# ScalarE's order in an opening attention, four weights loaded together, and query groups moved nearer to their keys

## The chip, the cores and the metric

The kernel runs on one core of one Trainium2 chip. Its time is the device time of one execution in microseconds (us). TensorE multiplies into PSUM banks (PE; PEld is its weight load), VectorE (DVE) and ScalarE (ACT) read the banks and work in SBUF, GpSimd (POOL) does little here, and SyncE (SP) issues most DMAs. Each engine takes its own instructions in a fixed order and waits at one until what it needs is there.

## The reference

Three stages follow one another: a linear attention over 4 batches of 8 heads, 576 positions and 64 dimensions, and two MLPs over the 2304 tokens.

```python
def phi(x):                                    # x: q or k of one head, w_phi 64x128
    proj = x @ w_phi
    proj = proj - max(abs(proj), axis=-1)
    return concat([exp(proj), exp(-proj)])     # 256 features
num = phi(q) @ (phi(k).T @ v);  den = phi(q) @ sum(phi(k)) + 1e-6
x = num / den                                  # heads side by side: 2304 x 512
h = x @ w_in;    x = max(0.01 * h, h) @ w_out  # 512 -> 2048 -> 512
g = x @ w_gate;  out = (silu(g) * (x @ w_val)) @ w_out2   # 512 -> 1536 -> 512
```

The inputs are laid out on the host, and the weights come as 64-bit floats of which a DMA brings the raw words.

## The kernel before

**Batches and units.** The work goes batch by batch. The MLPs of a batch are a list of units, each of 24 matmuls or so (`u_l1`, `u_out`, `u_gate`, `u_val`); the attention of batch b + 1 is mixed into the units of batch b. Only the attention of batch 0 has nothing to be mixed into. It is the opening, and it is what the change is about: TensorE, ScalarE and VectorE work on it alone, with a few weight conversions and the first matmuls of the first units, which can start before the last quarter of x is there.

**The opening.** Heads go in pairs, j = 0 to 3. The keys of a pair come in three groups (`first_k`: two matmuls per 128 positions into one bank, VectorE's largest absolute value L434, VectorE's difference, and on ScalarE the two exponentials L439 and L440). Then `first_back` multiplies them with the values into one bank (L218), and at the pair's last group ScalarE copies that bank to SBUF as `kvh` (`k_z`, L63). The queries of a pair come in two halves t of 288 positions, so there are eight query groups: `q_p` (projection L332, and VectorE's transposed maximum L337), `q_m_t` (a transposition L349 and a short chain on VectorE that ends in the row of maxima L362), `q_exp` (L372 subtracts it in the bank, ScalarE's exponentials L374 and L375, for two heads), `q_num` (L392, two matmuls per head with `kvh`, after which ScalarE takes the denominator `dn`, L395), and `q_fin` (VectorE: transpose L400, reciprocal L402, transpose L404, two products L410 to `xf`; then ScalarE's rounding to `xh`, L63, and VectorE's rest `xl`). x of the batch is there when the `xl` of the eighth group is written.

**Weights.** A weight tile takes three steps. `w_load` brings 512 KB into one of five `wi` buffers. `w_to_f32` makes a 32-bit float of it: on ScalarE L563 and L564, on VectorE L572, L573 and L578. `w_split` rounds it on ScalarE (L588) and takes the rest on VectorE (L60). The result is again a `wi` tile (first layer) or a `wo` tile (second layer). `split_next` does this for the next weight in the order of need, with two conversions and up to five loads ahead. The order of need is: four weights of the first layer, then the first of the second layer, the fifth of the first layer, and the other three of the second layer for the first `u_out`.

**What sets the order.** The program calls the steps of the opening in the order of the times that `first_steps` gives them, but a scheduler then orders the instructions of each engine by its own estimates. A stamp (`stamp_issue_order_token`) keeps the instructions that carry the same token in the order of the program. In the kernel before, the rounding of weights, the matmuls of units and some loads are stamped, and nothing of the opening is.

## Time and profile before

| | us |
|---|---|
| median of 3 runs (lowest, highest) | 1082.61 (1078.01, 1087.24) |
| the profiled execution | 1085.46 |
| its span, first to last instruction | 1083.5 |
| mean granted clock of TensorE in it | 0.987 of full speed |

The profiled execution is 2.85 us above the median. Rows of a timeline give the start in us, the length in us, engine and line, what is written and read, how many instructions were merged into the row, and in brackets how long the engine had sat idle and for whom. A row that merges several pipelined instructions is longer than the time until the next one starts. A 32-bit matmul leaves two records. Windows give busy us of each engine in a stretch, instructions in brackets, and the share of full speed that TensorE's clock was granted.

### The profile page before, as it was taken

What the parts mean: (1) busy time and instruction counts of PE and PEld (TensorE: products, weight loads), DVE (VectorE), ACT (ScalarE), POOL (GpSimd) and SP (SyncE); (2) the same over time, 40 slices, a digit from 0 to 9 for tenths busy, and PEclk for the clock granted to TensorE, in tenths of its full rate; (3) what the DMA queues carried; (4) which work ended last, traced back from release to release, by engine and by line L of the source; (5) the groups of instructions that cost most, each with busy time, mean ns of one, the idle gap of its engine ahead of it and who ended that gap; (6) DMA issues with size and microseconds to landing.
All of it is one profiled execution on the core that took longest, in us unless ns stands there. A gap on an engine that the chain in (4) does not pass through costs nothing.

```text
span 1083.5 us, 20399 instructions
## 1 busy us (share of the span) xinstructions
PE 1052.4 (97%) x7642; PEld 1025.2 (95%) x7642; DVE 795.2 (73%) x1730; ACT 648.9 (60%) x1443; POOL 21.7 (2%) x57
## 2 busy tenths in 40 slices
PE   8689999999999999999999999999999999999998
PEld 7579999998989999999999989999999999999998
DVE  5876778899898988968686855958878732368473
ACT  4656979788887787756563466754544334336541
POOL 1000100000000000000000000000000000000000
PEclk9699999999999999999999999999999999999999
DMA  7523677657665786786463385536977757657542
GB/s 221 182 60 125 223 261 257 235 186 243 211 230 192 287 341 239 262 305 238 164 224 127 121 318 205 186 117 258 320 250 280 287 193 275 219 175 273 207 141 86
DMA packets 101490, 236.17 MB, mean 218 GB/s; under 512 B 19856, under 2 KB 35984, under 8 KB 101392
## 3 DMA queue, kind: packets, MB, share of 16 engines
q1 hardware_dynamic: 94560, 219.41, 58.4%
q0 software_dynamic: 4032, 14.68, 3.4%
q8 instruction: 60, 0.98, 0.4%
q10 hardware_dynamic: 2800, 0.79, 0.3%
q14 instruction: 38, 0.31, 0.1%
HBM read 169.30 MB, written 65.54 MB: 217 GB/s over the span
## 4 chain that ended last, share of the span: by engine, by line
PE 61%; DMA 6%; DVE 3%; ACT 2%; issue 1%; SPq 0%; DVEq 0%
PE pm L652 42%; PE pa L778 8%; PE pm L778 4%; PE pa L392 2%; PE pa L230 2%; DMA wi<-parts 1%; DMA wi<-in_w_dram 1%; DMA wr<-kept 1%; PE pa L177 1%; DMA sums<-wr 1%; DMA wi<-in_wg_dram 0%; DMA vhl<-parts 0%; PE pa L372 0%; DVE xl L60 0%; PE pa L271 0%
## 5 line engine op out<-in xcount | busy, mean ns | idle before, releaser
L652 PE MATMUL pm<-xh,wi 128*128 128x288 f32 x1664 | 354.6, 300 | 3.1 <-DVE wi L60 1.0
L652 PE MATMUL pm<-gp,wo 128*128 128x288 f32 x2256 | 339.3, 296 | 1.5 <-ACT es L680 0.6
L652 PEld LDWEIGHTS pm<-gp,wo 128*128 128x128 f32 x2256 | 311.8, 188 | 3.4 <-ACT es L680 1.1
L652 PEld LDWEIGHTS pm<-xh,wi 128*128 128x128 f32 x1664 | 271.9, 188 | 7.7 <-DVE wi L60 2.2
L652 PE MATMUL pm<-xl,wi 128*128 128x288 f32 x832 | 246.5, 297 | 0.0
L652 PEld LDWEIGHTS pm<-xl,wi 128*128 128x128 f32 x832 | 156.7, 188 | 0.7
L719 DVE TENSOR_TENSOR acc<-pm,acc 128x288 f32<-128x288 f32 x160 | 70.2, 451 | 46.6 <-PE pm L652 45.8
L60 DVE TENSOR_TENSOR gp<-es,gp 128x576 fp32r<-128x576 f32 x94 | 70.4, 749 | 26.1 <-ACT gp L63 25.6
L63 ACT ACTIVATE gp<-es 128x576 fp32r<-128x576 f32 x94 | 64.6, 687 | 29.5 <-DVE es L700 24.4
L60 DVE TENSOR_TENSOR wi<-wr,wi 128x512 fp32r<-128x512 f32 x96 | 64.9, 683 | 12.0 <-ACT wi L588 11.3
L588 ACT ACTIVATE wi<-wr 128x512 fp32r<-128x512 f32 x96 | 60.0, 636 | 17.9 <-DVE wr L60 5.1
L778 PE MATMUL pm<-xh,wi 128*128 128x288 f32 x272 | 62.5, 296 | 2.1 <-DMA wi<-parts 1.2
L563 ACT ACTIVATE wr<-wi 128x512 f32<-128x512 f32 x68 | 46.3, 686 | 22.4 <-DMA wi<-in_w_dram 11.4
L60 DVE TENSOR_TENSOR fl<-ff,fh 128x512 fp32r<-128x512 f32 (+1 forms) x72 | 51.1, 712 | 11.2 <-ACT fh L63 10.8
L564 ACT ACTIVATE wi<-wi 128x512 int32<-128x512 uint32 x68 | 46.8, 688 | 18.2 <-DMA wi<-in_w_dram 12.4
L578 DVE TENSOR_TENSOR wr<-wr,wi 128x512 uint16<-128x512 uint16 x68 | 51.0, 750 | 0.8
L778 PEld LDWEIGHTS pm<-xh,wi 128*128 128x128 f32 x272 | 46.4, 188 | 3.2 <-DVE mk L182 1.2
L395 ACT ACTIVATE dn<-pa 64x288 f32<-64x288 f32 x64 | 26.0, 407 | 38.0 <-PE pa L392 37.2
L63 ACT ACTIVATE fh<-ff 128x512 fp32r<-128x512 f32 (+1 forms) x72 | 47.2, 659 | 0.9
L680 ACT ACTIVATE es<-pm 128x288 f32<-128x288 f32 x72 | 29.7, 418 | 27.2 <-PE pm L778 16.6
L63 ACT ACTIVATE acc<-pm 128x288 f32<-128x288 f32 x64 | 26.7, 431 | 25.5 <-PE pm L652 25.3
L700 DVE SCALAR_TENSOR_TENSOR es<-pm,es 128x288 f32<-128x288 f32 x72 | 32.2, 448 | 11.6 <-PE pm L652 11.1
(212 smaller groups left out, 2083.3 us busy)
## 6 DMA issues: line engine op xcount, KB each, us to landing
wo<-parts SPq DMA_DIRECT2D x77, 512.0 KB, 6.1
wi<-parts SPq DMA_DIRECT2D x68, 512.0 KB, 6.0
parts<-wi SPq DMA_DIRECT2D x56, 512.0 KB, 4.5
wi<-in_w_dram SPq DMA_DIRECT2D x44, 512.0 KB, 4.4
wr<-kept SPq DMA_DIRECT2D x64, 256.0 KB, 4.2
parts<-wo POOLq DMA_DIRECT2D x28, 512.0 KB, 5.4
kept<-wr SPq DMA_DIRECT2D x40, 256.0 KB, 4.5
wi<-in_wg_dram SPq DMA_DIRECT2D x12, 512.0 KB, 4.3
```

The lines of the kernel that those rows point to most:

```text
L60: dve.tensor_tensor(out=o, in0=a, in1=b, op=ALU.subtract)
L63: act.activation(o, a, AF.Copy)
L395: act.activation(dn[b, j, t][D * h : D * h + D], ps[D:P], AF.Copy, bias=1e-6)
L563: act.activation(t, high.bitcast(F32), AF.Abs, scale=REBIAS)
L564: act.activation(low, low.bitcast(U32), AF.Copy, scale=2.0**-29)
L578: dve.tensor_tensor(out=t16, in0=t16, in1=e16, op=ALU.add)
L588: i = act.activation(t[:, 0], r, AF.Copy)
L652: m = pe.matmul(ps, w, x[:, c], start=(i == 0), stop=(i == n - 1))
L680: act.activation(o, i, AF.Prelu, alpha=0.01)
L700: dve.scalar_tensor_tensor(out=g[:, c], in0=ps, scalar=0.5, in1=g[:, c], op0=ALU.mult, op1=ALU.mult)
L719: dve.tensor_tensor(out=acc[o][:, t], in0=ps, in1=acc[o][:, t], op=ALU.add)
L778: m = pe.matmul(ps, a, b, start=start and n == 0, stop=stop and n == 5, skip_group_check=True)
```

## The change

Instructions of ScalarE in the opening get one token, `opening`: every copy, exponential and denominator of the attention, and the first instruction of each weight conversion (L563 before, L570 now). So ScalarE takes these in the program's order. The second instruction of a conversion (L564, now L572) gets none. The first four weights are loaded together behind the last queries, with none further ahead, and each `split_first` converts and splits one weight; four are converted in the opening. The program's times are moved: the keys' products come 1.1 steps sooner after their exponentials, the query groups start one step earlier and follow at 1.3 steps, and their own steps lie nearer together. The first queries and the constants are loaded ahead of the second keys.

```diff
--- before.py
+++ after.py
@@ -59,8 +59,14 @@
     def sub(o, a, b):
         dve.tensor_tensor(out=o, in0=a, in1=b, op=ALU.subtract)
 
+    opening = [True]
+
+    def in_opening(i):
+        if opening[0]:
+            tc.stamp_issue_order_token(i.ins, "opening")
+
     def cp(o, a):
-        act.activation(o, a, AF.Copy)
+        in_opening(act.activation(o, a, AF.Copy))
 
 
     cst_sb = const.tile([P, NC], F32, name="cst_sb")
@@ -162,7 +168,8 @@
         v = vraw.pop((b, j))
         vhl[b, j] = t = T([P, NST, 2, 2, D], F32R, "vhl", 1)
         for st in (slice(0, 2), slice(2, NST)):
-            cp(t[:, st, :, 0, :], v[:, st])
+            i = act.activation(t[:, st, :, 0, :], v[:, st], AF.Copy)
+            tc.stamp_issue_order_token(i.ins, "opening")
             sub(t[:, st, :, 1, :], v[:, st], t[:, st, :, 0, :].bitcast(F32))
 
     def k_front(b, j, s):
@@ -371,8 +378,8 @@
         r = mrow[b, j][:, NB * t : NB * t + NB].rearrange("p k i -> p (k i)")
         pe.matmul(ps, sel[:, h], r, start=False, stop=True, skip_group_check=True)
         f = T([P, 2, HT], F32, "ff" if b else ("ff", "fh", "fl")[(2 * t + h + j) % 3], 3)
-        act.activation(f[:, 0], ps, AF.Exp)
-        act.activation(f[:, 1], ps, AF.Exp, scale=-1.0)
+        in_opening(act.activation(f[:, 0], ps, AF.Exp))
+        in_opening(act.activation(f[:, 1], ps, AF.Exp, scale=-1.0))
         if whole(b):
             qfh[b, j, h, t] = f
             return
@@ -392,7 +399,7 @@
             pe.matmul(ps, w, x, start=(i == 0), stop=(i == len(ops) - 1))
         if h == 0:
             dn[b, j, t] = T([P, HT], F32, "dn", 2)
-        act.activation(dn[b, j, t][D * h : D * h + D], ps[D:P], AF.Copy, bias=1e-6)
+        in_opening(act.activation(dn[b, j, t][D * h : D * h + D], ps[D:P], AF.Copy, bias=1e-6))
 
     def q_fin(b, j, t):
         d = dn.pop((b, j, t))
@@ -436,8 +443,8 @@
         d = f.rearrange("p n h a f -> p (n h) a f")
         m = mk.rearrange("p (r o) -> p r o", o=1).to_broadcast([P, 2 * n, F])
         sub(d[:, :, 1], pv, m)
-        act.activation(d[:, :, 0], d[:, :, 1], AF.Exp)
-        act.activation(d[:, :, 1], d[:, :, 1], AF.Exp, scale=-1.0)
+        in_opening(act.activation(d[:, :, 0], d[:, :, 1], AF.Exp))
+        in_opening(act.activation(d[:, :, 1], d[:, :, 1], AF.Exp, scale=-1.0))
         for i in range(n):
             ff[0, j, s + i] = f[:, i]
 
@@ -456,15 +463,15 @@
 
         for i, (j, s, n) in enumerate(pairs):
             at(i, first_k, j, s, n)
-            at(i + 2.5, first_back, j, s, n)
+            at(i + 1.4, first_back, j, s, n)
         for g in range(2 * NP):
             j, t = divmod(g, 2)
-            base = 3 + 1.25 * g
-            last = max(base + 2.4, 3 * j + 4.6 + 0.4 * t)
+            base = 2 + 1.3 * g
+            last = max(base + 2.05, 3 * j + 3.5 + 0.4 * t)
             at(base + 0.1, q_p, 0, j, t)
-            at(base + 0.9, q_m_t, 0, j, t)
+            at(base + 0.7, q_m_t, 0, j, t)
             for h in range(2):
-                at(base + 1.5 + 0.2 * h, q_exp, 0, j, h, t)
+                at(base + 1.25 + 0.1 * h, q_exp, 0, j, h, t)
                 at(last + 0.2 * h, q_num, 0, j, h, t)
             at(last + 0.25, q_fin, 0, j, t)
         steps = [[] for _ in range(int(max(e[0] for e in events)) + 1)]
@@ -560,7 +567,8 @@
         low, high = r[:, :, 0], r[:, :, 1]
         t = T([P, 512], F32, "wr", 4)
         ti = t.bitcast(I32)
-        act.activation(t, high.bitcast(F32), AF.Abs, scale=REBIAS)
+        i = act.activation(t, high.bitcast(F32), AF.Abs, scale=REBIAS)
+        tc.stamp_issue_order_token(i.ins, "opening")
         act.activation(low, low.bitcast(U32), AF.Copy, scale=2.0**-29)
         if key[0] in "gv3":
 
@@ -1072,6 +1080,10 @@
         for k in slots[i]:
             split_next()
 
+    def split_first():
+        ahead(conv, w_to_f32, done[0] + 1)
+        ahead(done, w_split, done[0] + 1)
+
 
     atts = {}
 
@@ -1093,27 +1105,29 @@
 
     warm_up()
     load_k(0, 0)
+    load_q(0, 0)
+    load_constants()
     load_k(0, 1)
-    load_q(0, 0)
+    load_q(0, 1)
     load_k(0, 2)
-    load_constants()
-    load_q(0, 1)
+    load_q(0, 2)
     load_k(0, 3)
-    load_q(0, 2)
     steps = first_steps()
 
     for i, todo in enumerate(steps):
         for fn in todo:
             fn()
-        if i == 2:
+        if i == 1:
             query_constants()
-        if i == 5:
+        if i == 4:
             load_q(0, 3)
-        if i in (6, 8, 10, 12):
-            split_next()
-        if i == 13:
+            ahead(loaded, w_load, 4)
+        if i in (4, 6, 8, 10):
+            split_first()
+        if i == 11:
             split_constants()
             load_k(1, 0)
+    opening[0] = False
     for i in range(NU):
         units[i]()
         splits(i)
```

Three places of ScalarE's order show what moves. Line numbers of the changed kernel are a few higher.

The first is ScalarE at the first query group, from its last exponentials to the next group's. `wr` and `wi` rows are conversions, `vhl` copies of values for the fourth batch, `dn` the first group's denominators, `wo` exponentials of keys. Before:

```order
L374 ACTIVATE fh_237<-pm_193 128x288
L375 ACTIVATE fh_237<-pm_193 128x288
L563 ACTIVATE wr_355<-wi_351 128x512
L564 ACTIVATE wi_351<-wi_351 128x512
L563 ACTIVATE wr_363<-wi_353 128x512
L564 ACTIVATE wi_353<-wi_353 128x512
L63 ACTIVATE vhl_4429<-vraw_3723 128x4x64
L588 ACTIVATE wi_371<-wr_355 128x512
L63 ACTIVATE vhl_4429<-vraw_3723 128x6x64
L395 ACTIVATE dn_257<-pa_254 64x288
L395 ACTIVATE dn_257<-pa_274 64x288
L374 ACTIVATE fl_292<-pm_220 128x288
```

Now:

```order
L381 ACTIVATE fh_216<-pm_184 128x288
L382 ACTIVATE fh_216<-pm_184 128x288
L69 ACTIVATE kvh_223<-pa_160 128x512
L572 ACTIVATE wi_293<-wi_293 128x512
L446 ACTIVATE wo_236<-wo_236 128x4x128
L447 ACTIVATE wo_236<-wo_236 128x4x128
L402 ACTIVATE dn_249<-pa_246 64x288
L402 ACTIVATE dn_249<-pa_251 64x288
L572 ACTIVATE wi_295<-wi_295 128x512
L572 ACTIVATE wi_297<-wi_297 128x512
L572 ACTIVATE wi_299<-wi_299 128x512
L69 ACTIVATE xh_264<-xf_261 128x288
```

The two conversions, the copies and the rounding that stood ahead of the two denominators are down to one conversion's second half and two exponentials; behind the denominators stand three more of those halves, and `xh` of this group stands ahead of the next group's exponentials.

The second is ScalarE at the last two query groups. Before:

```order
L395 ACTIVATE dn_705<-pa_702 64x288
L564 ACTIVATE wi_808<-wi_808 128x512
L395 ACTIVATE dn_705<-pa_707 64x288
L374 ACTIVATE fl_689<-pm_638 128x288
L375 ACTIVATE fl_689<-pm_638 128x288
L374 ACTIVATE ff_693<-pm_641 128x288
L375 ACTIVATE ff_693<-pm_641 128x288
L395 ACTIVATE dn_746<-pa_743 64x288
L63 ACTIVATE xh_720<-xf_717 128x288
```

Now:

```order
L69 ACTIVATE kvh_699<-pa_589 128x512
L381 ACTIVATE ff_702<-pm_655 128x288
L382 ACTIVATE ff_702<-pm_655 128x288
L572 ACTIVATE wi_779<-wi_779 128x512
L402 ACTIVATE dn_708<-pa_705 64x288
L402 ACTIVATE dn_708<-pa_710 64x288
L69 ACTIVATE xh_723<-xf_720 128x288
L402 ACTIVATE dn_730<-pa_727 64x288
L402 ACTIVATE dn_730<-pa_732 64x288
```

Before, half of the tenth conversion (`wi_808`) stood behind the first of the last four denominators; now half of the fifth (`wi_779`) stands ahead of all four.

The third is ScalarE in the first units, where the fifth weight of the first layer is rounded (`wi_816`). Before:

```order
L189 ACTIVATE ff_881<-pa_877,mk_879 128x128
L680 ACTIVATE es_888<-pm_889 128x288
L680 ACTIVATE es_763<-pm_778 128x288
L588 ACTIVATE wi_816<-wr_795 128x512
L588 ACTIVATE wo_870<-wr_810 128x512
L588 ACTIVATE wo_926<-wr_864 128x512
L588 ACTIVATE wo_1000<-wr_920 128x512
L680 ACTIVATE es_832<-pm_847 128x288
```

Now:

```order
L570 ACTIVATE wr_864<-wi_804 128x512
L572 ACTIVATE wi_804<-wi_804 128x512
L196 ACTIVATE ff_1119<-pa_1115,mk_1117 128x128
L688 ACTIVATE es_960<-pm_975 128x288
L570 ACTIVATE wr_920<-wi_806 128x512
L572 ACTIVATE wi_806<-wi_806 128x512
L596 ACTIVATE wi_816<-wr_789 128x512
```

Conversions of five weights (`wi_779` to `wi_806`), which lay in the opening, now stand in the units, and ahead of that rounding: between the last `xh` and it there are 35 instructions, where there were 10.

VectorE's conversions follow ScalarE's. Loads of weights stand on SP's queue behind those of the last queries: four at once, where two were, and the fifth waits until a conversion has freed its buffer.

## Rows read from the trace of the kernel before

**Rows 1.** The page: busy time of TensorE over the span.

```profile
PE 1052.4 (97%) x7642; PEld 1025.2 (95%) x7642; DVE 795.2 (73%) x1730; ACT 648.9 (60%) x1443; POOL 21.7 (2%) x57
```

**Rows 2.** Windows: length, busy us by engine, granted clock, DMA share, GB/s.

```profile
0.00:96.00 96.00, 78.68 (x386) 64.93 (x387) 66.96 (x168) 52.09 (x117) 5.21 (x23) 0.86 0.45 137
22.00:32.00 10.00, 10.00 (x64) 8.74 (x63) 8.82 (x23) 8.41 (x21) 0.00 (x0) 1.00 0.62 211
32.00:51.00 19.00, 10.22 (x27) 6.77 (x26) 17.22 (x40) 11.05 (x24) 0.31 (x1) 0.58 0.50 165
51.00:83.00 32.00, 27.91 (x151) 23.12 (x150) 24.31 (x63) 18.54 (x45) 1.50 (x4) 0.93 0.19 54
96.00:135.00 39.00, 39.00 (x297) 38.53 (x296) 29.32 (x61) 35.22 (x93) 5.09 (x12) 1.00 0.67 223
```

**Rows 3.** Timeline of TensorE, in the opening and at the first second-layer unit.

```profile
25.59 1.13 PE L392 MATMUL pa<-fh,kvh 128*128 128x288 f32 x4
...
35.62 2.29 PE L392 MATMUL pa<-ff,kvh 128*128 128x288 f32 x4 [3.04 <-ACT kvh L63]
...
42.96 0.85 PE L372 MATMUL pm<-acc,sel 128*128 128x288 f32 x2 [3.03 <-DVE acc L362]
...
110.32 0.96 PE L652 MATMUL pm<-gp,wo 128*128 128x288 f32 x6
```

**Rows 4.** Timeline of ScalarE around the first query group.

```profile
22.30 0.69 ACT L563 ACTIVATE wr<-wi 128x512 f32<-128x512 f32 x1
...
24.55 0.46 ACT L63 ACTIVATE vhl<-vraw 128x256 fp32r<-128x256 f32 x1
...
26.15 0.41 ACT L395 ACTIVATE dn<-pa 64x288 f32<-64x288 f32 x1
26.76 0.41 ACT L395 ACTIVATE dn<-pa 64x288 f32<-64x288 f32 x1 [0.20 <-PE pa L392]
```

**Rows 5.** Timeline of VectorE: the closing steps of three query groups.

```profile
30.38 0.46 DVE L400 STREAM_TRANSPOSE t<-dn 128x288 f32<-128x288 f32 x1
...
35.51 0.90 DVE L410 TENSOR_TENSOR xf<-pa,rb 64x288 f32<-64x288 f32 x2
...
70.34 0.48 DVE L400 STREAM_TRANSPOSE t<-dn 128x288 f32<-128x288 f32 x1 [0.44 <-ACT dn L395]
...
71.62 0.93 DVE L410 TENSOR_TENSOR xf<-pa,rb 64x288 f32<-64x288 f32 x2
...
93.44 0.90 DVE L410 TENSOR_TENSOR xf<-pa,rb 64x288 f32<-64x288 f32 x2
...
95.19 0.46 DVE L60 TENSOR_TENSOR xl<-xf,xh 128x288 fp32r<-128x288 f32 x1
```

**Rows 6.** Timeline of ScalarE in the second half of the opening.

```profile
70.33 0.63 ACT L439 ACTIVATE wo<-wo 128x512 f32<-128x512 f32 x1
...
72.54 0.43 ACT L375 ACTIVATE fl<-pm 128x288 f32<-128x288 f32 x1
72.83 0.46 ACT L63 ACTIVATE xh<-xf 128x288 fp32r<-128x288 f32 x1
...
78.76 0.60 ACT L63 ACTIVATE kvh<-pa 128x512 f32<-128x512 f32 x1 [0.46 <-PE pa L218]
```

**Rows 7.** Instructions by form, 0 to 96 us: count, busy us, mean ns, idle before.

```profile
L578 DVE TENSOR_TENSOR wr<-wr,wi 128x512 uint16<-128x512 uint16 x9 | 6.6, 736 | 0.0
L573 DVE SCALAR_TENSOR_TENSOR wr<-wi,wr 128x512 int32<-128x512 int32 x9 | 6.1, 677 | 0.1
L572 DVE TENSOR_SCALAR wr<-wr 128x512 int32<-128x512 int32 x9 | 3.6, 402 | 1.9 <-ACT wr L563 1.9
...
L588 ACT ACTIVATE wi<-wr 128x512 fp32r<-128x512 f32 x4 | 2.5, 626 | 1.1 <-DVE wr L578 1.0
```

**Rows 8.** Timeline of ScalarE: a conversion and the exponentials behind it.

```profile
44.79 0.67 ACT L564 ACTIVATE wi<-wi 128x512 int32<-128x512 uint32 x1 [2.15 <-DMA wi<-in_w_dram]
45.48 0.41 ACT L374 ACTIVATE fh<-pm 128x288 f32<-128x288 f32 x1
```

**Rows 9.** The page: issues of a weight load, KB each, median us to landing.

```profile
wi<-in_w_dram SPq DMA_DIRECT2D x44, 512.0 KB, 4.4
```

## The prediction

> **What bounds the kernel now.** I read the page's busy times first: TensorE is busy 97% of the span [rows 1], so time can only be won where it is not. The windows, read next, put that place in the opening. From 96 to 135 us it is busy in all 39 us at full clock; in the first 96 us it is busy 78.68, at a mean clock of 0.86; and the worst stretch is 32 to 51 us, 10.22 of 19 us at 0.58 [rows 2]. The reader is to see that VectorE is busy 17.22 us of these 19, while in the stretches on either side TensorE has 10.00 of 10 and 27.91 of 32 us.
>
> TensorE's timeline says what it waits for there: 3.04 us for the copy `kvh`, and 3.03 us for the row of maxima [rows 3]. Both come late because ScalarE and VectorE are converting weights. On ScalarE the copies and conversions from 22.30 to 26.15 us stand between the first group's exponentials and its denominators [rows 4]. On VectorE the first group's close takes from 30.38 to 36.41 us, 6.03 us, where an undisturbed one takes 70.34 to 72.55, 2.21 us [rows 5]. So the first `xf` ends at 36.41 us, the eighth at 94.34; the last `xl`, with which x is there, ends at 95.65 [rows 5].
>
> **The change part by part.** The sum is made against the profiled execution, 1085.46 us, which is 2.85 above the median of 1082.61; that is taken off at the end.
>
> *The first group comes sooner.* ScalarE's exponentials of the group end at 22.3 us now; I leave that, though its queries and constants are loaded earlier. Then follow `kvh` (0.60 us, [rows 6]), to 22.9, and on TensorE two pairs of products of at most 1.13 us each [rows 3], to 24.0 and 25.1. Meanwhile ScalarE does one half of a conversion, 0.56 us (four from 22.30 to 24.55, [rows 4]), and two exponentials of keys, 1.3 us, to 24.8. The second denominator ends at about 25.6 (0.41 each, [rows 4]). VectorE's order has the closing steps together, so 2.21 us on, at 27.8, `xf` is ready: 36.41 - 27.8 = 8.6 us sooner.
>
> *The period of the groups.* Seven periods follow. Before, they took (93.44 - 35.51) / 7 = 8.28 us each [rows 5]. In the new order of ScalarE the `xh` of a group stands ahead of the next group's exponentials, and these ahead of its denominators. That makes a ring: `xh` 0.46, exponentials of keys and queries 2.64 (70.33 to 72.97), `kvh` 0.60 in every second group [rows 6], two pairs 2.26, a denominator 0.41 [rows 3, 4], the close 2.21 [rows 5]: 7.98 without `kvh`, 8.58 with it, 8.28 in the mean. One weight in two groups adds half a conversion and a rounding, 0.56 + 0.63 [rows 4, 7], at most 0.6 per group, so 8.28 to 8.9, and I take the middle, 8.6: 7 x 0.32 = 2.2 us later. The nearest rows give other ends. VectorE has 66.96 us of work in the first 96 us [rows 2], of which five conversions leave, each (6.6 + 6.1 + 3.6) / 9 = 1.8 us [rows 7]: 57.9 us, 7.2 per group, and no period can be shorter for long. The upper end is in TensorE's clock. [...]
>
> *The last two groups.* Half a conversion now stands on ScalarE ahead of the last four denominators. Its load can be issued only when the fourth weight's conversion has freed a buffer, just before the last row of maxima; it lands 4.4 us later [rows 9]. Before, the last denominators began about 4 us after the last row of maxima. So I count 1 us, and bound it by 0 and 2.2, the longest such wait [rows 8].
>
> That such a wait holds everything behind it the trace shows: the half conversion at 44.79 us waited 2.15 us for its load, and the exponentials behind it, whose product had ended at 43.81 [rows 3], began at 45.48 [rows 8]. [...]
>
> *The weights left for later.* Nine conversions lay in the first 96 us [rows 7]; now four do, and four splits where there were five. That moves 10 x 0.56 + 0.63 = 6.2 us of ScalarE's work and 5 x 1.8 + 0.7 = 9.7 us of VectorE's behind the opening, where ScalarE was busy 35.22 of 39 us [rows 2]. Between the last `xh` and the rounding of the fifth weight it has 35 instructions of 35.22 / 93 = 0.38 us each [rows 2], 13.3 us, and the rounding ends at 13.9. TensorE needs that weight for the fifth unit. Its second-layer work began 14.7 us after x was there (110.32, [rows 3], less 95.65), one unit of some 3.2 us later, so it needs it at 11.5: 2.4 us of waiting. [...]
>
> *What costs nothing.* Four loads behind the last queries are 1 MB more before anything else; the halves of conversions that need them stand behind 25 us, and the loads of keys for the next batch are used only after the opening. VectorE now waits for a constant ahead of its first difference; ScalarE's first exponential has to wait for its table anyway, and without that cover a late constant would take as much off the 8.6.
>
> *Sum.* -8.6 + 2.2 + 1 + 2.4 = -3.0: 1082.5 in the profiled execution, 1079.6 at the median, say **1080**.
>
> **The rivals.** All are given at the median.
>
> *VectorE's pace.* If waits overlap and the period falls to 7.2 us, seven periods save 7.6 on top of 8.6, and the sum is -16.2 + 1 + 2.4 = -12.8: 1069.8. For it speaks that TensorE, without conversions ahead of the attention, was busy 87% of the time from 51 to 83 us [rows 2]; against it that ScalarE's order now closes the ring. Chance 0.22.
>
> *The clock stays low.* Slower: at 9.8 us per group the seven periods cost 10.6, and -8.6 + 10.6 + 1 + 2.4 = +5.4: 1088. Its place is TensorE's wait for the maxima in each group, and it decides from a period of 9.0 us on, where 7 x 0.74 eats the 5.2 that the other terms leave. For it speaks that the clock was low in the stretch with 3 us waits; against it that TensorE recovers when work has piled up, as from 51 us. Chance 0.14.
>
> *The fifth weight late.* With 8.5 us instead of 2.4 the sum is +3.1: 1085.7, slower also; it decides from 5.4 us of waiting on. For it speaks ScalarE's load after the opening, against it that TensorE never waited there before. Chance 0.14. Both together give +11.5, 1094; chance 0.08.
>
> *The change doesn't do what it says.* The second half of each conversion carries no token, and three of them stand ahead of the first `xh`. If that is the old jam again, it costs 3 x 0.56 = 1.7 us [rows 4], once: 1081.3, inside the forecast.
>
> **How the numbers follow.** The forecast has 0.42. Faster or slower by over 1%, 10.8 us, is about what a measurement of this kernel can tell from no change. Faster takes nearly all of the first rival, 0.2; slower the two late mechanisms together and a little of the clock alone, 0.1; the rest, 0.7, is within 1%. The range goes from 1067, the first rival with no price for the weights, to 1093, just short of both late mechanisms.
>
> **What would show it.** In the changed profile the first `xf` should end near 28 us, the following ones every 8.6 us, the last near 88 and the last `xl` near 90. [...] ScalarE should wait for `wi` once ahead of the last four denominators, and TensorE for `wi` before the fifth unit, 2 to 3 us. After that no wait should differ. A period near 7.2 makes the first rival right, one near 10 the second, and a wait of over 5 us at the fifth weight the third. A first `xf` after 32 us would make the whole forecast wrong.

## The result, and the profile after

The changed kernel takes 1095.60 us (median of 4 runs, 1093.98 to 1097.21), against 1082.29 before (4 runs): ratio 1.0121, interval 1.0075 to 1.0167. It is slower by 1.2%. The profiled execution takes 1097.21 us, 11.75 more than the one before.

The windows of the changed kernel, in the stretches of [rows 2], and one more:

```profile
0.00:96.00 96.00, 77.20 (x359) 62.80 (x360) 54.84 (x138) 42.56 (x94) 4.54 (x22) 0.86 0.33 98
22.00:32.00 10.00, 9.56 (x60) 8.39 (x59) 7.43 (x23) 7.00 (x15) 0.00 (x0) 1.00 0.14 39
32.00:51.00 19.00, 12.92 (x59) 10.49 (x59) 13.93 (x34) 9.68 (x23) 0.31 (x1) 0.84 0.07 22
51.00:83.00 32.00, 24.71 (x102) 18.41 (x101) 18.16 (x44) 10.98 (x26) 0.83 (x3) 0.77 0.09 26
96.00:135.00 39.00, 35.94 (x241) 34.30 (x240) 32.31 (x72) 34.12 (x91) 3.45 (x8) 0.91 0.72 253
...
110.00:123.00 13.00, 10.17 (x54) 9.19 (x53) 11.80 (x25) 12.49 (x32) 1.43 (x4) 0.75 0.95 343
```

The stretch that was worst before, 32 to 51 us, is better: 12.92 us busy for 10.22, at 0.84 for 0.58. The one behind it is worse: 24.71 of 32 us at 0.77, where [rows 2] have 27.91 at 0.93. And neither of the engines that TensorE waits for is busy there: VectorE has 18.16 of 32 us, ScalarE 10.98. All three idle in turn: they wait for one another, as the waits below show.

The mean clock of the opening is no lower than before: 0.86 in the first 96 us of both kernels. What has changed is where it is low: before mostly in the one stretch of the jam, now in several groups behind it.

VectorE's timeline, the rows that answer to [rows 5]: first and last `xf`, last `xl`.

```profile
26.13 0.89 DVE L417 TENSOR_TENSOR xf<-pa,rb 64x288 f32<-64x288 f32 x2
...
99.58 0.93 DVE L417 TENSOR_TENSOR xf<-pa,rb 64x288 f32<-64x288 f32 x2
...
101.68 0.46 DVE L60 TENSOR_TENSOR xl<-xf,xh 128x288 fp32r<-128x288 f32 x1 [1.17 <-ACT xh L69]
```

The first `xf` ends at 27.02 us, 9.4 sooner than before. The seven periods take 73.45 us, 10.49 each, where they took 8.28; the last `xl` ends at 102.14, 6.5 later.

ScalarE's waits, by what was waited for (us in total, times, longest), one line of the kernel before and three of the changed one:

```profile
ACT xh L63 <- DVE xf L410: 3.7, 2, 2.5
...
ACT xh L69 <- DVE xf L417: 16.1, 7, 3.3
ACT dn L402 <- PE pa L399: 12.3, 7, 3.8
ACT wo L446 <- DVE wo L60: 10.8, 7, 3.0
```

The second line is new in kind: in the kernel before ScalarE waited for `xf` twice, 3.7 us in all, behind the next group's exponentials. Now it stands at `xh` in seven of eight groups, with the next group's exponentials behind it. One turn of ScalarE's timeline, from the fourth `xh` to the next group's first denominator:

```profile
59.97 0.44 ACT L69 ACTIVATE xh<-xf 128x288 fp32r<-128x288 f32 x1 [2.38 <-DVE xf L417]
...
61.61 0.69 ACT L570 ACTIVATE wr<-wi 128x512 f32<-128x512 f32 x1
64.76 0.63 ACT L596 ACTIVATE wi<-wr 128x512 fp32r<-128x512 f32 x1 [2.46 <-DVE wr L586]
...
66.53 0.58 ACT L69 ACTIVATE kvh<-pa 128x512 f32<-128x512 f32 x1
69.75 0.41 ACT L402 ACTIVATE dn<-pa 64x288 f32<-64x288 f32 x1 [2.65 <-PE pa L399]
```

And TensorE's, with the start of the second layer (to be held against [rows 3]):

```profile
48.34 0.85 PE L379 MATMUL pm<-acc,sel 128*128 128x288 f32 x2 [2.06 <-DVE acc L369]
48.99 3.62 PE L225 MATMUL pa<-xl,wo 96*128 96x128 f32 x16
52.40 2.13 PE L399 MATMUL pa<-ff,kvh 128*128 128x288 f32 x4
...
60.70 0.54 PE L379 MATMUL pm<-acc,sel 128*128 128x288 f32 x2 [2.41 <-DVE acc L369]
...
65.44 1.30 PE L339 MATMUL pm<-raw,wbd 128*128 128x288 f32 x2 [1.96 <-DVE wo L60]
...
67.58 2.13 PE L399 MATMUL pa<-fl,kvh 128*128 128x288 f32 x4
69.51 2.13 PE L399 MATMUL pa<-ff,kvh 128*128 128x288 f32 x4
...
118.07 0.61 PE L660 MATMUL pm<-xh,wi 128*128 128x288 f32 x1 [0.70 <-ACT wi L596]
...
119.19 1.65 PE L660 MATMUL pm<-gp,wo 128*128 128x288 f32 x6
```

Behind the waits of 2.06 and 1.96 us pairs of products take 2.13 us, not 1.13: the granted clock is 0.50 from 48.4 to 55.0 us, and 0.50 again from 65.4 to 72.0 us, where the pairs at 67.58 and 69.51 run. ScalarE's next denominator waits for them, VectorE's close for that, and the next `xh` for the close.

The 11.75 us, in the order of the prediction's sum: first group -9.4; seven periods 73.45 - 57.93 = +15.5; from the last `xf` to the last `xl` +0.3; from there to the first second-layer matmul 17.05 us instead of 14.67, +2.4; the rest +2.9. Of the rest, 2.5 are there by the first copy of a second-layer result (130.09 us, before 118.69): TensorE is busy all the time in both stretches, 10.90 us from 119.19 and 8.37 before, but at a mean clock of 0.80 and 1.00. So the clock is worth some 10.90 x 0.20 = 2.2 of the 2.5 us, an estimate; the row at 119.19 has 1.65 us for what took 0.96 [rows 3]. And in the 17.05 us TensorE idles 2.83, where it idled nowhere before: 1.17 for `pk` from GpSimd, 0.96 for ScalarE's exponentials, 0.70 for the fifth weight's rounding (the row at 118.07).

### The profile page after: what moved, and what is told of

It is laid out like the page before. It is cut to its first block, busy times and chain, and to the rows that moved or that the text cites. A ratio compares the mean times of both kernels' runs of the same rounds, so it can differ in the third digit from the quotient of the medians.

```text
span 1095.3 us, 20408 instructions
## 1 busy us (share of the span) xinstructions
PE 1059.4 (97%) x7642; PEld 1031.3 (94%) x7642; DVE 798.1 (73%) x1730; ACT 650.7 (59%) x1443; POOL 21.8 (2%) x57
## 4 chain that ended last, share of the span: by engine, by line
PE 80%; DMA 6%; DVE 4%; ACT 2%; issue 1%; SPq 0%; DVEq 0%; ACTq 0%
PE pm L660 56%; PE pa L786 8%; PE pm L786 4%; PE pa L399 3%; PE pa L184 2%; PE pa L237 2%; PE pa L225 1%; DMA wi<-in_w_dram 1%; DMA wi<-in_wg_dram 1%; DMA wo<-parts 1%; DMA wi<-parts 1%; DMA wr<-kept 1%; DMA sums<-wr 1%; DMA vhl<-parts 1%; PE pa L379 0%
## 5 line engine op out<-in xcount | busy, mean ns | idle before, releaser
L60 DVE TENSOR_TENSOR gp<-es,gp 128x576 fp32r<-128x576 f32 x94 | 70.5, 750 | 25.9 <-ACT gp L69 25.2
L572 ACT ACTIVATE wi<-wi 128x512 int32<-128x512 uint32 x68 | 46.4, 685 | 17.7 <-DMA wi<-in_wg_dram 9.4
L570 ACT ACTIVATE wr<-wi 128x512 f32<-128x512 f32 x68 | 46.4, 683 | 15.6 <-DMA wi<-in_w_dram 5.8
L708 DVE SCALAR_TENSOR_TENSOR es<-pm,es 128x288 f32<-128x288 f32 x72 | 31.9, 447 | 12.8 <-PE pm L660 12.3
```

What stands on the lines that cost most here:

```text
L60: dve.tensor_tensor(out=o, in0=a, in1=b, op=ALU.subtract)
L570: i = act.activation(t, high.bitcast(F32), AF.Abs, scale=REBIAS)
L572: act.activation(low, low.bitcast(U32), AF.Copy, scale=2.0**-29)
L708: dve.scalar_tensor_tensor(out=g[:, c], in0=ps, scalar=0.5, in1=g[:, c], op0=ALU.mult, op1=ALU.mult)
```

## The experiments

The theory after this reading: the stamp on `xh` closes a ring through all engines, TensorE waits in it, and its clock falls with the waits (0.50 behind those of 2.06 and 1.96 us). The rivals: the moved times or loads, and the weights left for later. "Second layer" is the start of the first matmul of `wo`; the last three columns are of one profiled execution each.

| kernel | median us | ratio to before, interval | first xf starts, us | period, us | second layer, us |
|---|---|---|---|---|---|
| before | 1082.3 to 1083.6 | | 35.5 | 8.28 | 110.3 |
| changed | 1095.60 | 1.0121 (1.0075 to 1.0167) | 26.1 | 10.49 | 119.2 |
| e1_no_token | 1076.47 | 0.9943 (0.9918 to 0.9968) | 28.8 | 7.99 | 100.2 |
| e3_times_only | 1074.54 | 0.9930 (0.9907 to 0.9953) | 31.4 | 7.15 | 98.3 |
| e5_xh_free | 1080.35 | 0.9972 (0.9950 to 0.9993) | 24.0 | 8.40 | 100.3 |
| e6_att_token | 1100.95 | 1.0166 (1.0116 to 1.0216) | 30.8 | 11.22 | 124.6 |
| e7_filler | 1096.08 | 1.0106 (1.0073 to 1.0139) | 26.7 | 9.79 | 113.9 |
| e10_xh_later | 1082.75 | 1.0001 (0.9979 to 1.0023) | 24.1 | 8.31 | 101.2 |
| e9_times_four | 1077.28 | 0.9938 (0.9919 to 0.9957) | 29.1 | 7.88 | 100.0 |
| e4_four_only | 1082.00 | 0.9982 (0.9963 to 1.0002) | 36.0 | 7.50 | 105.2 |
| e16_after_eight | 1114.29 | 1.0283 (1.0253 to 1.0314) | 24.0 | 13.94 | 137.4 |
| e15_eight | 1098.20 | 1.0154 (1.0105 to 1.0203) | 24.0 | 11.63 | 121.2 |
| e12_first_token | 1075.73 | 0.9925 (0.9896 to 0.9954) | 25.2 | 8.27 | 97.8 |
| e14_later_free_next | 1085.76 | 1.0022 (1.0003 to 1.0041) | 24.0 | 9.81 | 109.3 |
| e17_link_alone | 1087.34 | 1.0045 (1.0015 to 1.0076) | 30.6 | 9.05 | 110.8 |
| e18_no_conv | 1091.06 | 1.0068 (1.0044 to 1.0091) | 24.2 | 8.67 | 112.2 |
| e19_no_conv_filler | 1095.41 | 1.0103 (1.0061 to 1.0145) | 26.8 | 9.17 | 118.3 |
| e11_later_free | 1076.63 | 0.9928 (0.9900 to 0.9956) | 26.0 | 8.50 | 100.4 |

**Which part of the change costs.** First, no stamps:

```diff
     def in_opening(i):
-        if opening[0]:
-            tc.stamp_issue_order_token(i.ins, "opening")
+        pass
```

(and none on L570 and `vhl`).

> The changed kernel without any of the new stamps: the program's times, its order of loads and its four first weights stay, but the scheduler is free again to order ScalarE (it brings up to nine conversions into the opening, as before). In the changed kernel the first xf ends at 27.0 us, the eighth at 100.5, a period of 10.49 us. Theory 1, ScalarE's fixed order closes a ring (xh, then the next exponentials, then the denominators, then the close) and TensorE's waits in it lower its clock: the period falls to 8.8 us or less, and the time to 1076 to 1086 us. Theory 2, the moved times or the loads bring the waits: the period stays at 10 us or more and the time at 1092 or more. Theory 3, only the weights left for later cost: the period stays, but the 5 us after the opening come back, about 1090.

The period fell to 7.99 us, the time to 1076.47. Then the other way round, times and loads alone, put into the kernel before:

```diff
-            base = 3 + 1.25 * g
-            last = max(base + 2.4, 3 * j + 4.6 + 0.4 * t)
+            base = 2 + 1.3 * g
+            last = max(base + 2.05, 3 * j + 3.5 + 0.4 * t)
```

> The kernel before with the moved times and the new order of loads alone; no stamps, and the conversions with up to five loads ahead as before, two steps sooner. Theory 1 (the fixed order costs): about as the kernel before or a little faster, 1074 to 1084 us, period at or under 8.6 us. Theory 2 (the moved times cost): 1090 us or more, with a period near 10 us. Theory 3 (the late weights cost): as before, 1078 to 1085.

1074.54 us, at the fast end. With these two, the moved times are not what costs: without stamps they gain 0.6 to 0.7%. Then the one link:

```diff
-        cp(xh[b, j][:, c], x)
+        act.activation(xh[b, j][:, c], x, AF.Copy)
```

> The changed kernel with the stamp taken from one link of the ring alone, ScalarE's rounding of x to xh: the scheduler now puts most of these behind the next group's exponentials. Theory 1: ScalarE no longer waits 2.2 to 3.3 us at xh ahead of exponentials whose product is there, which is worth about 1 us in each group and more where TensorE keeps its clock: period 9.0 to 9.7 us, time 1086 to 1091 us. Rival, the ring is held elsewhere (the rounding of a weight ahead of the keys' exponentials and kvh, and the products at half clock): the period stays above 10 us and the time at 1093 or more.

More came back than expected: 1080.35 us, period 8.40. ScalarE's wait at `xh` there:

```profile
ACT xh L422 <- DVE xf L417: 1.6, 3, 1.1
```

1.6 us in three waits, where the changed kernel has 16.1 in seven. The stamp on conversions, taken away alone, makes it worse:

```diff
-        tc.stamp_issue_order_token(i.ins, "opening")   # after L570
```

> The changed kernel with the stamp taken from the conversions alone: attention keeps the program's order on ScalarE, but the scheduler may put conversions where it likes, and it again brings nine of them into the opening, most between exponentials and denominators. Theory 1 with the attention's order at fault: the period stays at 10 us or more, time 1092 to 1100 us, or worse, since VectorE has five conversions more to do. Rival, the conversions' fixed place is at fault (ScalarE waits 2.46 us for a weight's rounding ahead of the keys' exponentials and kvh): period 9 to 9.6 us, time 1085 to 1090.

1100.95 us: the scheduler puts the conversions of four weights and three of their roundings ahead of the first `xh`, VectorE's part of them stretches the first group's close (its `xf` ends at 31.75 us), and TensorE then waits 7.32 us for the second group's exponentials, which stand behind that `xh`. So the stamps on conversions protect the attention; it is `xh` that hurts. To see whether that takes the scheduler's freedom, all stamps stay and the program calls the rounding later:

```diff
+            at(last + 0.7, q_round, 0, j, t)    # cp to xh and the rest xl, out of q_fin
```

> The changed kernel with all of its stamps, but the rounding xh and the rest xl are called by the program 0.45 steps after the group's close, so that they stand behind the next group's exponentials. Theory 1, one link closes the ring: as with the stamp taken from xh alone (8.40 us, 1080), period 7.8 to 8.7 us, time 1074 to 1083. Rival, the whole fixed order is too rigid and the scheduler's freedom was what helped there: period above 9.5 us and 1088 or more.

The period is 8.31 us, as expected; the time 1082.75, at the upper end. The place of `xh` in the order decides, not who sets it. And the link alone, in the kernel with the times alone:

```diff
+        tc.stamp_issue_order_token(i.ins, "link")   # q_exp: both exponentials; q_fin: xh; b == 0
```

> The kernel before with the moved times and loads (1074.54 us, period 7.15 us, no stamps), and one link alone stamped: the rounding xh of a group keeps its place ahead of the exponentials of the next group's queries, as in the changed kernel. Denominators, exponentials of keys, kvh and conversions stay free. If this link is the cause, the period rises to 9.5 us or more and the time to 1088 or more. If the link needs the rest of the fixed order to hurt (keys' exponentials, kvh, the rounding of weights in the ring), the period stays under 8.6 us and the time under 1083.

1087.34 us, 12.8 more than without it; the period rises by 1.9 us to 9.05, less than the 9.5 expected. The waits for `xf`:

```profile
ACT xh L416 <- DVE xf L411: 6.4, 6, 2.7
```

So the link alone takes away all that the moved times gain and some more, but the rest of the fixed order adds to it in the changed kernel.

**What makes the ring long.** TensorE gets something to do in its waits (a token keeps these matmuls between the transposition and the subtraction):

```diff
+    w = wbd.rearrange("p h c -> p (h c)")[:, 0:224]
+    for _ in range(4):      # between q_m_t's transposition and q_exp's product
+        pe.matmul(pt[b, j, 0, t][:, HT : HT + 224], wbd[:, 0], w, start=False, ...)
```

> The changed kernel with TensorE given something to do in its waits: behind each group's transposition, ahead of the subtraction of its row of maxima, it does four matmuls of 224 columns more, into columns of a bank that nobody reads (they serve nothing but this test; some 0.42 us each at full clock, 1.7 us per group, from 0.54 us for two records of 288 columns). ScalarE's order in the opening stays the same but for four conversion halves and roundings. Theory 1 has two parts, the ring and the clock that falls in its waits. If the clock makes the step from the 8.6 us worked out at full speed to 10.49 us, the stretches at 0.6 to 0.85 between 33 and 85 us go, and the period falls to 8.6 to 9.4 us although TensorE has 1.7 us per group more to do: 1082 to 1090 us. If the ring is as long without the clock, the period stays at 10.3 us or more and the time at 1095 to 1105.

Windows from 33 to 80 us, of the kernel before, the changed kernel and this one:

```profile
33.00:80.00 47.00, 35.92 (x163) 28.27 (x163) 37.60 (x93) 27.04 (x60) 1.81 (x5) 0.78 0.28 82
33.00:80.00 47.00, 34.45 (x137) 26.28 (x136) 28.71 (x70) 19.01 (x44) 1.14 (x4) 0.78 0.08 24
33.00:80.00 47.00, 37.53 (x196) 30.28 (x194) 31.71 (x76) 20.85 (x50) 1.15 (x4) 0.96 0.10 29
```

A miss for both numbers of the period: the clock is back at 0.96 from 33 to 80 us (0.78 in the changed kernel), but the period only falls to 9.79, and the time stays at 1096.08. Then no conversions in the ring, without and with the filler:

```diff
-        if i in (4, 6, 8, 10):
-            split_first()
...
+    for _ in range(4):      # behind the opening
+        split_first()
```

> The changed kernel with its four conversions called after the opening instead of within it; ScalarE's order of the attention is the same. The units then wait for their weights, so the opening is what is read, not the total. The conversions were counted at up to 0.6 us per group. If that is right, the period falls from 10.49 to about 9.9 us; if the waits that they bring count too (2.46 us for a rounding ahead of kvh in the fifth group), to 8.6 to 9.3; if they cost nothing, it stays at 10.3 to 10.6.

> The same without conversions in the opening, and with the four filler matmuls per group in TensorE's waits (they serve nothing else). What is left is the ring alone at full clock, which was worked out as 8.0 to 8.6 us. If the ring was rightly counted, the period is 8.0 to 8.8 us; if steps were left out of it (the keys' products on TensorE and their maxima on VectorE stand behind the row of maxima, some 2.4 us), it is 9.2 us or more.

The same windows, of the kernel without conversions:

```profile
33.00:80.00 47.00, 35.39 (x171) 26.89 (x172) 25.78 (x67) 22.01 (x54) 1.10 (x4) 0.93 0.07 17
```

and with the filler as well:

```profile
33.00:80.00 47.00, 38.12 (x202) 31.43 (x201) 27.89 (x71) 19.08 (x46) 1.14 (x4) 0.96 0.08 19
```

The four periods make a table:

| | conversions in the ring | none |
|---|---|---|
| TensorE waits idle | 10.49 | 8.67 |
| with filler | 9.79 | 9.17 |

e18 came out where the waits that the conversions bring count too, e19 between its two: the filler's own place in the ring costs 9.17 - 8.67 = 0.5 us or more, which the expectation hadn't counted. With the filler, the conversions add 9.79 - 9.17 = 0.62 us per group. Without it they add 10.49 - 8.67 = 1.82. The difference, 1.2 us, is put down here to the clock, which is 0.50 behind two of TensorE's waits in the changed kernel, where a pair of products takes 2.13 us and not 1.13. That takes the filler to cost 0.5 us with conversions too. If it costs nothing in the longer waits there, the clock is worth 10.49 - 9.79 = 0.70 and the conversions up to 1.12. So the clock's part is 0.7 to 1.2 us per group, from periods of one execution each, and the kernel without conversions isn't quite at full clock either (0.93 from 33 to 80 us).

The ring alone is not long: without conversions it takes 8.67 us, and with conversions but `xh` called later (e10) a period takes 8.31, both near the 8.28 of the kernel before. The 2 us come only where both meet.

**What the weights left for later cost.** Four weights alone, in the kernel before, and with the moved times:

```diff
-            split_next()
+            split_first()      # and ahead(loaded, w_load, 4) behind the last queries
```

> The kernel before with the four first weights loaded together and converted singly with none ahead, alone: old times, old order of loads, no stamps. The jam of conversions at the first group should be smaller: first xf before 33 us (35.5 before), last xf by 92 us or sooner (93.4 before), time 1076 to 1082. If the late weights cost more than the lighter opening gives: 1083 to 1088.

> The kernel before with the moved times, the new order of loads, and the four first weights loaded together and converted singly with none ahead; no stamps. It differs from the run with the times alone (1074.5 us, period 7.15) in the weights. If weights left for later cost 2.4 us, as the prediction had it, or up to 5 with what follows them, this is 1077 to 1080; if they cost nothing, 1073 to 1076; if VectorE's lighter opening pays, the last xf comes sooner than 81.5 us and the time is 1070 to 1073.

Neither prices what it was meant to: without stamps the scheduler pulls the later conversions into the opening all the same. The first `xf` of e4 is no sooner (36.0 us). Its second layer starts 5.1 us sooner and its time is the same; where those 5 us went these runs don't show. e9 loses 2.6 us against e3 within the opening (its last `xl` ends at 86.3 us, e3's at 83.7), not behind it (13.7 us from there to the second layer, e3 14.7). Four conversions more in the opening, in one lot:

```diff
+        if i == 10:
+            ahead(loaded, w_load, 8)
+            ahead(conv, w_to_f32, 8)
```

> The changed kernel with four more weights loaded and converted in the opening, in one lot at its tenth step; ring, stamps and everything else stay. It prices the weights left for later. In the changed kernel's profiled execution the time from the last xl (102.1 us) to the end was 995.1 us, in the kernel before 989.8. If the conversions left for later cost these 5.3 us, the last xl comes 0 to 4 us later here (2.2 us of ScalarE's and 7 us of VectorE's work stand in the opening, where both have idle time), and the rest falls to 986 to 990 us: time 1088 to 1094. If they cost nothing (the 5 us come from something else, such as the lower clock at the first units), the rest stays at 994 to 996, and the time at 1095 to 1100.

> The kernel with xh called later (1082.75 us; last xl at 84.9 us, rest 998.1 us) with the same four conversions more in its opening. If weights left for later are where the gain of the shorter opening went, the rest falls to 986 to 991 us, and with an xl up to 4 us later the time is 1073 to 1079. If not, the rest stays near 998, and the time is 1082 or more.

Both failed as a price and showed another one, in ScalarE's timeline of the first:

```profile
86.88 0.66 ACT L570 ACTIVATE wr<-wi 128x512 f32<-128x512 f32 x1 [3.67 <-DMA wi<-in_w_dram]
...
93.00 0.66 ACT L570 ACTIVATE wr<-wi 128x512 f32<-128x512 f32 x1 [2.77 <-DMA wi<-in_w_dram]
...
99.87 0.66 ACT L570 ACTIVATE wr<-wi 128x512 f32<-128x512 f32 x1 [5.66 <-DMA wi<-in_w_dram]
...
106.01 0.66 ACT L570 ACTIVATE wr<-wi 128x512 f32<-128x512 f32 x1 [4.92 <-DMA wi<-in_w_dram]
```

Each load waits for a buffer that the conversion before it frees (the last three are there 4.89, 5.66 and 4.92 us after that conversion's end), so four loads lie in series on ScalarE, 17.0 us of waiting, ahead of the last two groups' denominators; the time rose by 18.7. What stands behind all four starts late: the last of the four conversions at 106.01 us, the next exponentials of queries at 108.00, the next denominator at 114.98. Better is to let the scheduler place the later ones, with `xh` called later:

```diff
-        tc.stamp_issue_order_token(i.ins, "opening")   # L570, always
+        in_opening(...)                                # only while the program is in the opening; vhl alike
```

> The kernel with xh called later (1082.75 us; last xl ends at 84.9 us, the first second-layer matmul starts 16.4 us later, at 101.2), with conversions stamped only while the program is in the opening: the scheduler may pull the fifth and later ones forward, and puts one or two of them ahead of the last xh. If the late fifth weight costs about 2.4 us as predicted, the second layer starts 14 us after x, and the time is 1078 to 1081. If the cost lies later, with ScalarE behind through the first units, 1076 to 1079; if nothing changes, 1082 to 1084.

1076.63 us, 6.1 less than e10 and in the range of the second expectation. The first row of the second layer in TensorE's timeline of e10:

```profile
101.21 1.65 PE L671 MATMUL pm<-gp,wo 128*128 128x288 f32 x6
```

and of e11:

```profile
100.41 0.97 PE L669 MATMUL pm<-gp,wo 128*128 128x288 f32 x6
```

Windows from 160 to 300 us, of e10:

```profile
160.00:300.00 140.00, 131.17 (x921) 125.40 (x919) 118.36 (x243) 114.76 (x235) 6.93 (x13) 0.99 0.65 220
```

and of e11:

```profile
160.00:300.00 140.00, 135.28 (x963) 130.96 (x962) 124.50 (x256) 118.98 (x244) 7.44 (x14) 0.99 0.69 232
```

With x there at 84.85 and 87.36 us, the second layer starts 16.4 and 13.1 us later: 3.3 us, of the size of the 2.4 predicted for the late fifth weight. But x comes 2.5 us later in e11, so the second layer starts only 0.8 us sooner, and most of the 6.1 us lies behind that: its first row takes 1.65 us in e10, as at 119.19 us in the changed kernel, where the granted clock is 0.50 up to 121.00 us, and 0.97 in e11; and e10 idles 4.1 us more between 160 and 300 us. With as many loads ahead as in the kernel before, the conversions in the fixed order come back as stalls:

```diff
-            split_first()
+            split_next()        # in e11's kernel
```

> The kernel with xh called later, with stamps on conversions only while the program is in the opening, and the conversions and loads ahead as in the kernel before (two and up to five). Attention stays in the program's order; eight conversions lie in the opening instead of four or five. Last xl at 85 to 88 us, rest 986 to 991 us: 1073 to 1078. Rival: conversions in a fixed place between exponentials and kvh stretch the groups (14.4 us in the fifth group of the changed kernel): last xl after 90 us, 1080 or more.

1085.76 us: the rival, a period of 9.81. Last, stamps for the first group's attention alone, in the kernel with the times alone (conversions keep theirs):

```diff
+        if i == 4:
+            opening[0] = False
```

> The kernel before with the moved times and loads (as in the run with the times alone: 1074.54 us, first xf at 31.4, period 7.15 us), and stamps on the attention until the first group's close alone, so that no conversion goes ahead of its denominators; after that the scheduler is free, with up to nine conversions in the opening. If the first group's place and the later period can be had apart from one another, the first xf ends by 27 us, the period stays at 7.2 to 8.0 us and the time is 1068 to 1074. If what was put off meets the second group, the period is 8 us or more and the time 1074 to 1080.

1075.73 us, the second expectation. The first `xf` came at 25.2, but the second group paid for it (38.69, a period of 13.5); the opening ends 1.3 us later than in e3. Versions e1, e3, e9, e11 and e12 are faster than both kernels by 0.6 to 0.75% of the time before, with intervals that overlap; what they share is that no stamp holds `xh` ahead of the next exponentials throughout. That isn't enough by itself: e4, e10 and e14 share it too and are as slow as the kernel before.

## Why the prediction was wrong

**The first group**: predicted 8.6 us sooner, measured 9.4. The mechanism held: the conversions no longer stand ahead of the first denominators. That the number came so near is in part luck. The exponentials end at 20.1 us, not at 22.3 as the sum left them, and the keys' exponentials ahead of the denominators then waited 1.27 us for VectorE, which it hadn't counted. And the moved times and loads alone give 4.1 of the 9.4 (e3). Three halves of conversions ahead of the first `xh` cost nothing, since `xh` waited for `xf` behind them (0.67 us).

**The period**: this is the step that failed, "at most 0.6 per group, so 8.28 to 8.9, and I take the middle, 8.6: 7 x 0.32 = 2.2 us later". It was 10.49, and 15.5 us. The ring was seen, and without conversions it measures 8.67 where 8.28 was worked out. What the conversions do in it was mis-sized: 1.82 us per group, not 0.3. By the table 0.6 to 1.1 of it is there with the filler's clock of 0.96, more than the middle that was taken. The rest, 0.7 to 1.2, is put down to the clock, which the sum put at nothing and left to a rival with 0.14. That rival's 9.8 us per group is the 8.6 of the sum and 1.2 for the clock, a term that no run shows: [rows 3] have one pair of products at 2.29 us behind a wait of 3.04 where another took 1.13, and a group has two pairs; in the fifth group of the changed kernel both took 2.13, and the period came to 10.49. The reason given against that rival, that TensorE recovers when work has piled up, came from the kernel before, from its stretch behind the jam: [rows 2] have the clock at 0.93 from 51 to 83 us, the changed kernel 0.77, with waits of TensorE of 2.41, 1.96 and 1.38 us in that stretch. What the prediction overlooked is that 8.28 was no full-clock period to start from: from 33 to 80 us the mean clock is 0.78 in the kernel before as well. That the ring, summed at full clock, came to the same 8.28 is chance, as far as the rows show. In the changed kernel the clock goes down and up again: 1.00 in the wait from 46.3 to 48.3 us, 0.50 from 48.4 to 55.0, 1.00 from 58.3 to 61.7, 0.50 from 62.2 to 72.0, 1.00 from 73 to 85.

**The last two groups**: 1 us was counted for the fifth weight's half conversion; it waited for nothing (at 91.48 us). The mechanism is real, though: four such loads kept ScalarE waiting 17.0 us in e16.

**The weights left for later**: 2.4 us predicted from x to the second layer, 2.4 measured. The number came out, the wait did not: TensorE was to wait 2 to 3 us for the fifth weight and waited 0.70, with 2.13 us more for other late results. What was missed is the clock of the unit behind these waits, 0.80 from 119.19 to 130.09 us: by the estimate above some 2.2 us more.

**The rivals**: "both together", the clock and the late weight, gave +11.5 us and 1094, with a chance of 0.08; what came was +11.75 and 1095.60. That these agree is mostly luck. The seven periods cost 15.5 us, not the 10.6 of that rival; the weights cost 2.4 to the second layer, 5.3 with all that follows, not its 8.5, which no run shows; and the first group gained 9.4, not 8.6. The second rival, the clock in the ring, named the right place. The third did not come by its own measure: it decides from 5.4 us of waiting at the fifth weight, and there were 0.70. The chances were too low where it mattered: each late mechanism had 0.22 in all and both together 0.08, little more than the 0.05 of independent ones. That TensorE's waits lead to both is argued here, not shown. The range ended at 1093, just short of what came.

**Left open**: what follows the first second-layer matmul. By the medians, less the start of the second layer in the profiled execution, it is 972.6 us for the kernel before, 976.2 to 977.9 for the versions that beat it and 980 to 982 for e5, e7 and e10. The traces tell where most of it lies for these three. Windows from 160 to 300 us, of the changed kernel and of e7:

```profile
160.00:300.00 140.00, 137.60 (x988) 132.37 (x987) 124.02 (x255) 116.51 (x242) 6.91 (x13) 1.00 0.66 223
160.00:300.00 140.00, 133.04 (x946) 128.38 (x945) 120.72 (x246) 113.96 (x236) 6.93 (x13) 0.99 0.66 221
```

TensorE is busy 137.6 us there in the changed kernel (137.0 before), 133.0 in e7, 131.2 in e10 and 131.0 in e5: 4 to 6 us more of waits. In e10 3.2 us of them are three waits of the next batch's query groups for ScalarE's exponentials. Why ScalarE is late there no run shows. And executions of one kernel differ by 9 us (e5: 1076.75 to 1085.90) and more (e17: 1084.16 to 1099.10), so one trace each doesn't settle the rest.

## What to carry to other kernels

Before fixing an engine's order, write down for each instruction in it what it waits for, and look at what stands behind: a result that nobody needs soon (`xh`, a rounding) placed ahead of what everybody needs (exponentials) turns a pipeline into a ring, and with conversions in it one stamp cost 15 us (1095.60 against 1080.35). Where a ring has TensorE waiting some 2 us in most turns, products as slow as those measured behind such waits here (2.13 us a pair, not 1.13, at a granted clock of 0.50) belong into the forecast itself, not into a rival. Not every such wait brings them: behind one of 2.17 us at 91.16 us in e19 the granted clock is 1.00 (90 to 100 us). And an experiment that moves work must be looked at in the order that results: four of these runs priced something else, because the scheduler pulled the work back, or because its loads had no free buffer.

## What was not expected of the hardware

In e16 conversions whose loads of 512 KB wait for their buffer follow one another on ScalarE by 6 to 7 us (starts at 86.88, 93.00, 99.87, 106.01), though a conversion is some 1.2 us of its work (two instructions of 0.66). And filling TensorE's waits with matmuls that serve nothing brought its clock from 0.78 to 0.96 (33 to 80 us) and the second layer 5.3 us forward, and yet gave nothing in the total (1096.08 against 1095.60); in the profiled executions TensorE waits 4.6 us more than in the changed kernel between 160 and 300 us (133.04 us busy against 137.60).
